# DMA transposes for the last batch's queries and two tiles of x, weight casts in blocks of 128 rows, and a new list of steps, in a fused linear-attention and highway kernel

## The chip, the core and the metric

The kernel runs on one core of a Trainium2 chip. The core has a matrix engine (TensorE, PE in the profile, with its weight loads as PEld), a vector engine (VectorE, DVE), an engine for activation functions (ScalarE, ACT), a general engine (GpSimd, POOL) and an engine that here only issues transfers (SyncE, SP). Each runs its own instructions in order, and semaphores order them against each other. Sixteen DMA engines move data between the large memory (HBM) and the on-chip SBUF. Matmul results land in PSUM.

The metric is the device time of one execution in microseconds (us), the median of several runs. The profile is of one further execution. It gives the span, from the first to the last instruction, which is a little shorter than the time.

## The reference

Linear attention over 8 batches of 8 heads, 576 positions and 64 columns a head, then a highway layer over 4608 tokens of 512 columns:

```python
def _attn_ref(q, k, v):
    q_s = np.exp(q - np.max(q, axis=-1, keepdims=True))
    q_s = q_s / (np.sum(q_s, axis=-1, keepdims=True) + 1e-09)
    k_s = np.exp(k - np.max(k, axis=2, keepdims=True))
    k_s = k_s / (np.sum(k_s, axis=2, keepdims=True) + 1e-09)
    kv = np.einsum('bhsd,bhse->bhde', k_s, v)
    return np.einsum('bhsd,bhde->bhse', q_s, kv).astype(np.float32)

def _moe_ref(x, w_h, w_t, b_t):
    H = np.maximum(x @ w_h, 0.0)
    T = 1.0 / (1.0 + np.exp(-(x @ w_t + b_t)))
    return (T * H + (1.0 - T) * x).astype(np.float32)
```

The attention's output, with its heads laid side by side, is the x of the second function. q, k, v, both 512x512 weights and the output are float32.

## The kernel before

The 4608 tokens are 36 tiles of 128 rows. Nine tiles belong to two batches: four to the first, four to the second, and one that holds the last 64 rows of each (tiles 8, 17, 26 and 35). So tiles 0 to 3 are batch 0, 4 to 7 batch 1, 27 to 30 batch 6 and 31 to 34 batch 7.

What is done is written out by hand: the string `ORDER` (L16 to L62) is a list of steps such as `mt_33_0`, where the first word is a function of the kernel, the numbers are its arguments and a letter behind a colon chooses an engine (A is ACT, D is DVE, P is POOL). The loop at the end (L491 to L494) calls the steps in this order. Each engine's own queue is therefore the list with the other engines' steps left out. Steps that only issue transfers go to SP, which takes them in order too: an issue that waits holds all issues behind it. A transfer on SP also waits for the one issued eight before it.

The steps that matter here:

- Loads: `q`, `k` and `v` of a batch, `w` (half a weight matrix, L207). Queries of batches 4 to 7 arrive in two transfers of 512 KB (`q_7_0`) and a small one for the 64 rows at the end (`q_7_9`).
- Batch steps: `ek` takes exp of k on ACT (L249) and `vc` casts v to fp16 (L255). `kv` multiplies them on PE (L261), `kr` and `kn` divide by the sums on DVE into a small matrix kvb. `eq` takes exp of the queries on ACT into a tile qe (L293). `qt` turns them on PE, with the rows on which the heads' columns then lie (L309), 8 transposes of 128x128 for two tiles of tokens, into PSUM; `qc` copies them to SBUF (L328). `turned_q` (L336) says where a tile's turned queries lie.
- Tile steps: `xu` multiplies the turned queries with kvb (L339), `rs` and `x` divide by the sums on DVE (L358, L363), which gives x in fp16. `xt` turns x on PE with four transposes (L370), `xe` copies it to SBUF (L378, DVE with D, else ACT). `bw` puts the bias into PSUM, by a matmul or, with A, by a copy on ACT (L385). `mt` and `mh` are four matmuls each with the weights t and h (L397, L405). `th` is the tanh on ACT (half the gate), `dd` is max(h, -x/2) on DVE (L428), `uu` multiplies the two, on DVE or as two instructions on POOL (L432), `oo` adds x on POOL (L453), `st` issues the store (L464).
- Weights: `whd` subtracts the identity from w_h in a block of 128 rows on POOL or DVE (L223), `whc` casts half of w_h at once with a factor 0.5 (L227), `wtc` half of w_t (L216). `fill` runs matmuls on zeros (L165).

PSUM holds two banks for gates (`ps_t`), two for h and for the halves of the first tiles (`ps_g`), one pair for kv and xu (`ps_x`) and one bank each for turned queries and turned x. So a step such as `xu` waits until `x` of the tile before has read its sums.

Of the kernel before, what the change touches and what calls it, by code (L numbers as in the profile page):

```python
# [16 lines left out]
b_0 q_0_0 v_0_1 setupdve k_0_0 b_32 eq_0_0 bsplit setuppool fill_5 fill_8 bp v_0_0 bc qt_0_0 ek_0_1 v_0_3 ek_0_0 k_0_2  # L17
v_0_2 vc_0_3:A bw_1 vc_0_0 ek_0_2 vc_0_2 q_0_4 vc_0_1:D ek_0_3 bw_0 w_h_0 fill_8 qc_0_0 whd_1:P kv_0_0 eq_0_1 w_h_2
w_t_2 kr_0_0 whd_0:P whd_2:P w_t_0 k_1_2 v_1_2 q_1_0 k_1_0 v_1_0 fill_5 q_1_4 kn_0_0 q_2_0 k_2_0 eq_0_2 xu_0_0 v_2_0
q_3_0 rs_0_0 whc_0:A x_0_0 k_3_0 fill_4 v_3_0 kv_0_1 fill_3 kr_0_1 kn_0_1 xu_0_1 rs_0_1 xu_1_0 rs_1_0 qt_0_1 x_1_0  # L20
whd_3:P qc_0_1 xt_1_0 xu_3_0 qt_0_2 xe_1_0:D fill_1 rs_3_0 x_3_0 x_0_1 xt_3_0 xu_2_0 wtc_2:P whc_2:A mh_1_0 wtc_0:P
vc_1_3 xe_3_0:D xt_0_0 xt_0_1 mh_3_0 qc_0_2:A xe_0_1 mt_1_0 mt_0_1 dd_1 ek_1_3 rs_2_0 xe_0_0:D mt_0_0 x_2_0 xt_2_0
vc_1_2:D mh_0_0 th_1_0 mh_0_1 uu_1_0 dd_3 ek_1_2 kv_1_1 dd_0 th_0_0 oo_1_0 kr_1_1 kn_1_1 bw_3 eq_1_0 bw_2 qt_1_0
uu_0_0:P xe_2_0 ek_1_1 qc_1_0 mt_3_0 xu_5_1 rs_5_1 mh_2_0 x_5_1 xt_5_1 ek_1_0 vc_1_1:A th_3_0 xe_5_1 dd_2 vc_1_0
xu_4_1 kv_1_0 mt_2_0 kr_1_0 rs_4_1 eq_1_1 bw_5 th_2_0 kn_1_0 xu_5_0 eq_1_2 q_4_0 x_4_1 rs_5_0 x_5_0 mt_5_1 xu_4_0
qt_1_1 qc_1_1:A oo_0_0 v_4_0 xt_5_0 xe_5_0:D mh_5_1 uu_3_0:P bw_4 mh_5_0 rs_4_0 x_4_0 xt_4_1 xe_4_1:D mt_5_0 uu_2_0:P
oo_2_0 eq_2_0:F th_5_0 xu_6_0 dd_5 xt_4_0 xe_4_0:D qt_1_2 mh_4_1 mt_4_1 mt_4_0 th_4_0 oo_3_0 mh_4_0 bw_8:A rs_6_0
uu_5_0:P bw_6:A qc_1_2 ek_2_0:F x_6_0 xt_6_0 xe_6_0:D oo_5_0 xu_8_0 qt_2_0 rs_8_0 mh_6_0 q_4_9 x_8_0 dd_4 xt_8_0
xe_8_0:D xu_7_0 rs_7_0 qc_2_0 x_7_0 mt_6_0 dd_6 mt_8_0 vc_2_2:A qt_2_1 th_6_0 xt_7_0 qc_2_1:A th_8_0 vc_2_0 kv_2_0
mh_8_0 xe_7_0:D uu_6_0 kr_2_0 kn_2_0 mh_7_0 k_4_0 eq_3_0:F xu_9_0 dd_8 uu_4_0:P k_5_0 bw_7 qt_2_2 v_5_0 rs_9_0 oo_4_0  # L30
x_9_0 mt_7_0 xt_9_0 dd_7 qc_2_2:A q_5_0 xu_10_0 xe_9_0:D bw_10:A th_7_0 rs_10_0 x_10_0 oo_6_0 qt_3_0 qc_3_0 mh_9_0
bw_9:A ek_3_0:F uu_8_0:P uu_7_0:P vc_3_0 xu_12_0 st_1_1 xt_10_0 oo_8_0 rs_12_0 x_12_0 xe_10_0:D oo_7_0 mt_9_0 dd_9
qt_3_1 vc_3_2:A xu_11_0 xt_12_0 rs_11_0 x_11_0 xe_12_0:D mt_10_0 th_9_0 th_10_0 kv_3_0 uu_9_0 oo_9_0 xt_11_0 mh_10_0
xe_11_0 kr_3_0 kn_3_0 dd_10 mh_12_0 qc_3_1 xu_14_0 rs_14_0 x_14_0 bw_12:A bw_11:A mt_12_0 mh_11_0 uu_10_0:P oo_10_0
xu_13_0 eq_4_0 eq_4_1 qt_3_2 st_1_0 xt_14_0 vc_4_0 mt_11_0 dd_12 rs_13_0 th_12_0 x_13_0 qc_3_2 uu_12_0:P bw_14:A
oo_12_0 xu_15_0 rs_15_0 x_15_0 xe_14_0 th_11_0 qt_4_0 dd_11 mt_14_0 uu_11_0 xt_13_0 xu_16_0 rs_16_0 qc_4_0:A xe_13_0
x_16_0 mh_14_0 qt_4_1 xt_15_0 th_14_0 bw_13:A xu_17_0 xe_15_0:D mt_13_0 rs_17_0 x_17_0 ek_4_0:F mh_13_0 xt_16_0 eq_4_2
vc_4_2 th_13_0 k_6_0 kv_4_0 dd_14 dd_13 xe_16_0:D kr_4_0 kn_4_0 bw_15:A uu_13_0 mh_15_0 ek_5_0:F bw_16:A oo_11_0
vc_5_2:A mt_15_0 th_15_0 q_5_9 qc_4_1 xu_18_0 rs_18_0 x_18_0 v_6_0 dd_15 uu_14_0:P mh_16_0 xt_17_0 xe_17_0:D qt_4_2
mt_16_0 th_16_0 vc_5_0 dd_16 kv_5_0 oo_14_0 oo_13_0 kr_5_0 kn_5_0 qc_4_2:A mh_17_0 xt_18_0 xe_18_0:D bw_17:A uu_16_0  # L40
q_6_0 mt_17_0 eq_5_0:F xu_20_0 rs_20_0 mh_18_0 st_5_0 qt_5_1 x_20_0 dd_17 xt_20_0 bw_18:A st_3_1 th_17_0 xu_21_0
st_3_0 xe_20_0:D mt_18_0 qc_5_1:A uu_15_0:P bw_20:A rs_21_0 oo_15_0 st_5_1 x_21_0 qt_5_0 xt_21_0 dd_18 q_7_0 v_7_0
th_18_0 bw_21:A st_7_1 oo_16_0 xu_19_0 ek_6_0 uu_17_0:P oo_17_0 xe_21_0:D ek_6_2 rs_19_0 mh_20_0 mh_21_0 vc_6_0:A
x_19_0 xt_19_0 qc_5_0 xe_19_0:D xu_22_0 st_7_0 rs_22_0 x_22_0 dd_20 k_7_0 dd_21 mt_20_0 th_20_0 mt_21_0 vc_6_2
uu_18_0:P xt_22_0 kv_6_0 xe_22_0:D eq_5_2 mh_19_0 bw_19:A mt_19_0 qt_5_2 kr_6_0 kn_6_0 th_21_0 uu_21_0 xu_23_0 qc_5_2
eq_6_0:F mh_22_0 st_16_1 uu_20_0:P qt_6_0 bw_22:A st_10_1 rs_23_0 x_23_0 xt_23_0 xu_24_0 st_10_0 dd_19 mt_22_0
xe_23_0:D oo_18_0 oo_20_0 th_19_0 rs_24_0 oo_21_0 x_24_0 uu_19_0:P bw_23:A dd_22 mt_23_0 oo_19_0 qc_6_0 xt_24_0
xe_24_0:D st_21_0 xu_25_0 mh_23_0 q_6_9 rs_25_0 th_22_0 uu_22_0:P oo_22_0 mh_24_0 x_25_0 xt_25_0 dd_23 xu_26_0 dd_24
rs_26_0 th_23_0 bw_24:A mt_24_0 x_26_0 eq_7_0:F uu_23_0:P qt_7_0 st_12_0 qc_7_0 xu_27_0 q_7_9 oo_23_0 rs_27_0 x_27_0
xe_25_0 mh_25_0 st_17_0 qt_6_1 qc_6_1 bw_25:A vc_7_2:A th_24_0 xt_26_0 xe_26_0:D vc_7_0:A mt_25_0 th_25_0 uu_24_0  # L50
xu_29_0 rs_29_0 x_29_0 bw_27:A st_12_1 mh_26_0 bw_26:A xt_27_0 xe_27_0:D qt_7_1 dd_25 xu_28_0 st_8_0 uu_25_0:P st_14_1
mt_26_0 rs_28_0 ek_7_0:F dd_26 mt_27_0 oo_24_0 x_28_0 xt_29_0 kv_7_0 xe_29_0:D xt_28_0 th_26_0 uu_26_0 oo_26_0 th_27_0
# [13 lines left out]
def kernel(  # L66
# [120 lines left out]
    MAIN = 4 * 2 * 4 * D  # L187

# [27 lines left out]
    def wt_cast(e, c):  # L216
        if e == "D":
            nc.vector.tensor_scalar_mul(w16["t"][:, c:c + 2], T[f"wt{c}"], 1.0)
        else:
            copy = nc.gpsimd.tensor_copy if e == "P" else nc.scalar.copy  # L220
            copy(w16["t"][:, c:c + 2], T[f"wt{c}"])  # L221
# [5 lines left out]
    def wh_cast(e, c):  # L227
        if e == "D":
            nc.vector.tensor_scalar_mul(w16["h"][:, c:c + 2], T[f"wh{c}"], 0.5)
        else:  # L230
            nc.scalar.mul(w16["h"][:, c:c + 2], T[f"wh{c}"], 0.5)
# [103 lines left out]

    def turned_q(b, jp, n):  # L336
        return T[f"eq{b}_{jp // 2}"][:, jp % 2, n]
# [16 lines left out]

    def sums(i, k):
        return T[f"xu{i}_{k}"][:, :, 0:260].rearrange("p k (s e) -> p k s e", s=4)
# [6 lines left out]
    def x(e, i, k):  # L363
        k0, k1 = heads(i, k)
        t = once(f"xn{i}", lambda: xp.tile([P, 2, 4, D], FP16, tag="x16", name=f"x16_{i}"))
        T[f"x{i}"] = t.rearrange("p k s e -> p (k s e)")
        nc.vector.tensor_mul(t[:, k0:k1], sums(i, k)[:, :, :, 0:64],  # L367
                             T[f"rs{i}_{k}"][:, 0:k1 - k0].unsqueeze(3).to_broadcast([P, k1 - k0, 4, D]))

    def xt(e, i, k):  # L370
        k0, k1 = heads(i, k)
        t = T[f"xtps{i}"] = turned[:, 0]
        for n in range(2 * k0, 2 * k1):
            n0 = n // 2 * 2 * P
            nc.tensor.matmul(t[:, n], T[f"x{i}"][:, n0 + n % 2:n0 + 2 * P:2], idh, is_transpose=True,  # L375
                             start=True, stop=True, skip_group_check=True)
# [20 lines left out]
    def mt(e, i, k):  # L397
# [3 lines left out]
        for n in parts:  # L401
            nc.tensor.matmul(T[gate(i, k)][:, cs], T[f"xT{i}"][:, n], w16["t"][:, n, cs], start=False,  # L402
                             stop=(n == parts[-1] and not first), skip_group_check=True)

    def mh(e, i, k):  # L405
# [3 lines left out]
        for n in parts:  # L409
            nc.tensor.matmul(t, T[f"xT{i}"][:, n], w16["h"][:, n], start=(first and n == parts[0]),  # L410
# [17 lines left out]
    def dd(e, i):  # L428
        t = T[f"d{i}"] = dp.tile([P, DM], FP16, tag="d16", name=f"d16_{i}")
        nc.vector.scalar_tensor_tensor(t, T[f"x{i}"], -0.5, T[f"gps{i}"], op0=ALU.mult, op1=ALU.max)  # L430
# [22 lines left out]
    def oo(e, i, h):  # L453
# [8 lines left out]
        eng.tensor_add(t[:, cs], T[f"u{i}_{h}"][:, cs], T[f"x{i}"][:, cs])  # L462
# [62 lines left out]
```

## Time and profile before

| what | value |
|---|---|
| median of 3 runs | 119.61 us (119.45 to 119.64) |
| profiled execution | 119.67 us |
| its span | 117.6 us |
| bytes moved | 40.06 MB (read 30.41, written 9.44) |
| the last real matmuls start at | 111.83 us |
| 128x512 matmuls of weights h and t, busy per instruction | 379 ns |
| transposes of 128x128 on PE, busy per instruction | 219 to 220 ns |
| qc, 128x1024 | 681 ns on DVE, 1013 on ACT |
| xe, 128x512 | 421 ns on DVE, 582 on ACT |
| x and dd, 128x512, on DVE | 690 and 678 ns |
| oo, 128x512, on POOL | 1157 ns |
| weight casts, 128x1024 | 1057 ns on ACT, 1039 on POOL |

Busy time of each engine and the load on the transfers in some stretches, as the trace gives it:

```profile
10.00:20.00 10.00, 7.79 (x94) 4.26 (x93) 7.04 (x20) 5.37 (x8) 4.47 (x7) 1.00 1.04 394
20.00:30.00 10.00, 9.34 (x131) 4.91 (x131) 7.00 (x18) 8.26 (x14) 6.92 (x9) 1.00 1.07 381
40.00:50.00 10.00, 9.83 (x152) 6.08 (x150) 9.40 (x23) 9.36 (x13) 9.70 (x11) 1.00 1.06 377
95.00:100.00 5.00, 5.00 (x39) 2.79 (x38) 4.53 (x10) 3.82 (x10) 4.84 (x6) 1.00 0.73 188
100.00:105.00 5.00, 5.00 (x41) 2.88 (x39) 4.44 (x11) 3.38 (x7) 4.83 (x7) 1.00 0.97 339
```

The columns are the stretch, its length, the busy us of PE, PEld, DVE, ACT and POOL with the number of instructions, the granted clock, the transfers' share of the sixteen engines (it can pass 1 by the way packets are counted) and GB/s. A matmul counts as busy until its modelled end, though the next one starts before it, so a PE that is busy all the time need not be at its limit; the distance between starts says more.

### The profile page before, as it was taken

To read this page: it belongs to the slowest core of one execution; us is meant where nothing else is said; L and a number is where in the kernel's file an instruction comes from. 1 tells how busy PE (TensorE), PEld (TensorE's weight loads), DVE (VectorE), ACT (ScalarE), POOL (GpSimd) and SP (SyncE) were. 2 spreads that over 40 slices of the span, in tenths; PEclk is the share of its full clock that TensorE was granted. 3 is DMA by queue.
4 is the path that set the end of the run, shared out by engine and by line. 5 is a ranking of instruction groups with operands and counts; after the bars stand their busy time and mean duration, and the time that the engine had idled before them with its cause. 6 is when DMAs were issued, how large, how long until landed. Compare 5 with 4: busy or idle time off the path is not lost.

```text
span 117.6 us, 3461 instructions
## 1 busy us (share of the span) xinstructions
PE 110.6 (94%) x1371; PEld 63.6 (54%) x1371; DVE 94.3 (80%) x223; ACT 92.3 (78%) x130; POOL 91.9 (78%) x103
## 2 busy tenths in 40 slices
PE   5999867989999999999999999999999999999991
PEld 1354443535655666556655566666666655554450
DVE  5654685588769899997899999889989898988870
ACT  4375481798999999799999999996998987774520
POOL 5022237299999999999999999899999789996860
PEclk9999999999999999999999999999999999999999
DMA  2999999999999999999999999999999977971595
GB/s 46 393 392 380 408 396 385 378 375 384 394 389 390 389 391 362 374 355 390 389 375 383 381 363 361 395 374 380 406 403 363 279 235 180 301 283 56 210 364 173
DMA packets 22083, 40.06 MB, mean 341 GB/s; under 512 B 3250, under 2 KB 9650, under 8 KB 22068
## 3 DMA queue, kind: packets, MB, share of 16 engines
q1 hardware_dynamic: 21920, 39.72, 94.8%
q8 instruction: 10, 0.16, 0.6%
q10 hardware_dynamic: 148, 0.14, 0.4%
q14 instruction: 5, 0.04, 0.1%
HBM read 30.41 MB, written 9.44 MB: 339 GB/s over the span
## 4 chain that ended last, share of the span: by engine, by line
PE 69%; DMA 17%; DVE 8%; SPq 2%; ACT 1%; issue 1%; DVEq 0%
PE gps L410 23%; PE tps L402 22%; DMA q<-in_q_dram 11%; PE xu L352 6%; DMA v<-in_v_dram 6%; PE turned L375 5%; PE kv L268 4%; DVE x L367 4%; PE qps L323 2%; PE qps L318 2%; SPq L183 2%; PE turned L167 2%; DVE d L430 2%; ACT qe L306 1%; DVE rs L361 1%
## 5 line engine op out<-in xcount | busy, mean ns | idle before, releaser
L462 POOL TENSOR_TENSOR o<-u,x 128x512 f32<-128x512 f16 (+1 forms) x36 | 40.7, 1144 | 3.7 <-DVE u L444 2.8
L402 PE MATMUL tps<-w16t,xT 128*128 128x512 f16 (+1 forms) x148 | 36.3, 373 | 0.8 <-POOL w16t L221 0.8
L410 PE MATMUL gps<-w16h,xT 128*128 128x512 f16 x144 | 36.3, 379 | 0.0
L367 DVE TENSOR_TENSOR x<-xu,rs 128x512 f16<-128x512 f32 (+1 forms) x39 | 25.2, 649 | 2.8
L442 POOL TENSOR_TENSOR u<-g,d 128x512 f16<-128x512 f16 x21 | 24.3, 1157 | 2.5 <-DVE rs L361 0.9
L430 DVE SCALAR_TENSOR_TENSOR d<-x,gps 128x512 f16<-128x512 f16 x36 | 24.2, 678 | 1.7 <-PE gps L410 1.6
L252 ACT ACTIVATE ek<-k 128x576 f16<-128x576 f32 (+2 forms) x15 | 18.0, 1222 | 2.5 <-DMA k<-in_k_dram 2.5
L402 PEld LDWEIGHTS <-xT 128*128 128x128 f16 x148 | 13.4, 98 | 12.1 <-issue 1.1
L410 PEld LDWEIGHTS <-xT 128*128 128x128 f16 x144 | 12.8, 98 | 11.4 <-DVE xT L382 0.5
L390 ACT COPY tps<-ball 128x512 f32<-128x512 f32 x28 | 16.3, 592 | 2.4 <-DVE u L444 2.1
L258 POOL CAST v<-v 128x1152 f16<-128x1152 f32 (+1 forms) x10 | 9.5, 953 | 10.4 <-DMA v<-in_v_dram 9.9
L375 PE MATMUL turned<-idh,x 128*128 128x128 f16 x144 | 14.3, 220 | 1.0 <-DVE x L367 1.0
L352 PE MATMUL xu<-kvb,eq 128*128 128x130 f16 (+1 forms) x160 | 14.8, 224 | 0.5 <-DVE eq L332 0.2
L167 PE MATMUL turned<-blank 128*128 128x512 f16 x44 | 12.5, 431 | 1.3 <-POOL blank L149 1.3
L352 PEld LDWEIGHTS <-eq 128*128 128x128 f16 (+1 forms) x160 | 10.2, 100 | 6.5 <-DVE x L367 1.3
L424 ACT ACTIVATE th<-tps 128x512 f16<-128x512 f32 x21 | 12.3, 592 | 1.6 <-PE tps L402 1.6
L375 PEld LDWEIGHTS <-x 128*128 128x128 f16 x144 | 10.1, 98 | 6.5 <-DVE x L367 2.6
L441 POOL TENSOR_SCALAR g<-th 128x512 f16<-128x512 f16 x21 | 13.1, 622 | 0.2 <-ACT th L424 0.2
L382 DVE COPY xT<-turned 128x512 f16<-128x512 f16 (+1 forms) x27 | 10.8, 399 | 2.8 <-PE turned L375 2.5
L306 ACT ACTIVATE qe<-q 128x1024 f16<-128x1024 f32 (+2 forms) x8 | 9.2, 1160 | 4.3 <-DMA q<-in_q_dram 4.1
L426 ACT ACTIVATE tps<-tps 128x512 f32<-128x512 f32 (+1 forms) x16 | 8.9, 556 | 2.9 <-PE tps L402 2.7
L444 DVE SCALAR_TENSOR_TENSOR u<-tps,d 128x512 f16<-128x512 f32 (+1 forms) x15 | 10.0, 669 | 0.8 <-ACT tps L426 0.2
(48 smaller groups left out, 114.6 us busy)
## 6 DMA issues: line engine op xcount, KB each, us to landing
k<-in_k_dram SPq DMA_DIRECT2D x6, 1152.0 KB, 11.6
v<-in_v_dram SPq DMA_DIRECT2D x6, 1152.0 KB, 14.4
out_dram<-o SPq DMA_DIRECT2D x23, 256.0 KB, 6.3
q<-in_q_dram SPq DMA_DIRECT2D x10, 512.0 KB, 9.5
out_dram<-o SPq DMA_DIRECT2D x6, 512.0 KB, 5.5
k<-in_k_dram SPq DMA_DIRECT2D x4, 576.0 KB, 11.9
q<-in_q_dram SPq DMA_DIRECT2D x2, 1152.0 KB, 15.6
q<-in_q_dram SPq DMA_DIRECT2D x2, 640.0 KB, 10.5
```

Of the source, the lines that this page charges most:

```text
L167: nc.tensor.matmul(spare, blank[:, 0:P], blank, start=True, stop=True, skip_group_check=True)
L252: nc.scalar.activation(t[:, :, c:c + n].rearrange("p j c d -> p c j d"), T[f"k32{b}"][:, c:c + n].rearrange("p c (j d) -> p c j d", j=NJ), ...
L352: nc.tensor.matmul(dst, turned_q(b, jp, n), kvb[b % NKV][:, hh, kk], start=True, stop=True, skip_group_check=True)
L367: nc.vector.tensor_mul(t[:, k0:k1], sums(i, k)[:, :, :, 0:64], T[f"rs{i}_{k}"][:, 0:k1 - k0].unsqueeze(3).to_broadcast([P, k1 - k0, 4, D]))
L375: nc.tensor.matmul(t[:, n], T[f"x{i}"][:, n0 + n % 2:n0 + 2 * P:2], idh, is_transpose=True, start=True, stop=True, skip_group_check=True)
L390: nc.scalar.copy(t[:, cs], ball[:, cs])
L402: nc.tensor.matmul(T[gate(i, k)][:, cs], T[f"xT{i}"][:, n], w16["t"][:, n, cs], start=False, stop=(n == parts[-1] and not first), skip_gro ...
L410: nc.tensor.matmul(t, T[f"xT{i}"][:, n], w16["h"][:, n], start=(first and n == parts[0]), stop=(n == parts[-1] and not (first and len(part ...
L430: nc.vector.scalar_tensor_tensor(t, T[f"x{i}"], -0.5, T[f"gps{i}"], op0=ALU.mult, op1=ALU.max)
L441: nc.gpsimd.tensor_scalar(g, T[f"th{i}"], 1.0, 1.0, op0=ALU.add, op1=ALU.mult)
L442: nc.gpsimd.tensor_mul(t, g, T[f"d{i}"])
L462: eng.tensor_add(t[:, cs], T[f"u{i}_{h}"][:, cs], T[f"x{i}"][:, cs])
```

## The change

Three parts:

- Batch 7's queries for tiles 31 to 34 are turned by two DMA transposes on SP (`qd`) straight from qe into SBUF, 128x1024 each, in place of `qt_7_0`, `qt_7_1` and their `qc`. They are cut by halves of qe, not by tiles, so `turned_q` looks elsewhere for batch 7. The small `qt_7_2` for tile 35 stays.
- x of tiles 32 and 33 is turned by a DMA transpose on SP (`xt_33_0:T`, `xt_32_0:T`), 128x512, in place of four PE transposes and the copy `xe`. For these tiles `x` writes its columns in another order in two DVE instructions, so that the blocks come out right; `dd` and `oo` read x through a view with a step of 256 elements, and `mt` and `mh` take the blocks in another order.
- `wtc` and `whc` cast one block of 128 rows (128x512) and are spread over POOL, ACT and DVE.

The list of steps is new throughout. Among other things it loads w_t ahead of w_h and batch 1's queries ahead of its k and v, runs `mt` of tiles 1, 3 and 0 ahead of `mh`, has fewer fills (26 in place of 44), more `vc` on POOL, fewer `uu` on POOL (18 in place of 21), and puts tile 6's bias on PE.

```diff
     def wt_cast(e, c):
-        if e == "D":
-            nc.vector.tensor_scalar_mul(w16["t"][:, c:c + 2], T[f"wt{c}"], 1.0)
-        else:
-            copy = nc.gpsimd.tensor_copy if e == "P" else nc.scalar.copy
-            copy(w16["t"][:, c:c + 2], T[f"wt{c}"])
+        copy = dict(D=nc.vector.tensor_copy, P=nc.gpsimd.tensor_copy).get(e, nc.scalar.copy)
+        copy(w16["t"][:, c], T[f"wt{c // 2 * 2}"][:, c % 2])
...
     def wh_cast(e, c):
...
+        mul = nc.vector.tensor_scalar_mul if e == "D" else nc.scalar.mul
+        mul(w16["h"][:, c], T[f"wh{c // 2 * 2}"][:, c % 2], 0.5)
...
+    def qd(e, b, g):
+        t = T[f"eq{b}_{g}"] = eqp.tile([P, 2, 4, P], FP16, tag="eq", name=f"eq_{b}_{g}")
+        half = MAIN // 2
+        nc.sync.dma_start_transpose(t.rearrange("p a n t -> p (a n) t"),
+                                    T[f"qe{b}"].rearrange("p j c d -> p (j c d)")[:, g * half:(g + 1) * half])
+
     def turned_q(b, jp, n):
+        if b in TURNED and jp < 4:
+            return T[f"eq{b}_{n % 2}"].rearrange("p a n t -> p (a n) t")[:, 2 * jp + n // 2]
         return T[f"eq{b}_{jp // 2}"][:, jp % 2, n]
...
+        if i in SPLIT:
+            flat = T[f"x{i}"].rearrange("p (r k s m) -> p k s m r", k=2, r=2, s=4)
+            for kk in range(2):
+                nc.vector.tensor_mul(flat[:, kk], sums(i, k)[:, kk, :, 0:64].rearrange("p s (m r) -> p s m r", r=2),
+                                     T[f"rs{i}_{k}"][:, kk].unsqueeze(2).unsqueeze(3).to_broadcast([P, 4, 32, 2]))
+            return
...
+        if e == "T":
+            t = T[f"xT{i}"] = xtp.tile([P, 4, P], FP16, tag="xT", name=f"xT_{i}")
+            nc.sync.dma_start_transpose(t, T[f"x{i}"])
+            return
...
-        nc.vector.scalar_tensor_tensor(t, T[f"x{i}"], -0.5, T[f"gps{i}"], op0=ALU.mult, op1=ALU.max)
+        nc.vector.scalar_tensor_tensor(shaped(i, t), natural(i), -0.5, shaped(i, T[f"gps{i}"]), op0=ALU.mult, op1=ALU.max)
...
+        if i in SPLIT:
+            eng.tensor_add(shaped(i, t), shaped(i, T[f"u{i}_{h}"]), natural(i))
+        else:
+            eng.tensor_add(t[:, cs], T[f"u{i}_{h}"][:, cs], T[f"x{i}"][:, cs])
```

The list's part around batch 7's queries and around the two tiles, after:

```
... eq_7_0:F v_7_0 xt_24_0 mh_23_0 x_25_0 xe_24_0:D xu_26_0 xt_25_0 bw_24:A mt_23_0 oo_19_0 qc_6_1 rs_26_0 qd_7_0 ...
... xu_33_0 rs_33_0 mt_28_0 th_28_0 x_33_0 oo_27_0 st_21_0 uu_29_0:P st_14_0 mt_31_0 uu_28_0 th_31_0 bw_30:A xt_30_0
qc_6_2:A oo_28_0 xu_32_0 st_8_0 xe_30_0:D mh_31_0 oo_29_0 rs_32_0 x_32_0 q_7_9 eq_7_2 st_23_0 dd_31 mh_30_0 xt_33_0:T
dd_30 st_17_0 uu_31_0:P oo_31_0 bw_33:A xu_34_0 qt_7_2 rs_34_0 x_34_0 qc_7_2:A xt_32_0:T st_26_0 mt_30_0 mh_33_0 ...
```

## The prediction

> **What bounds the kernel now.** I read the page's busy line and slices first, then the chain that ended last in order of time, then the stretches, then each engine's timeline at both ends of the span.
>
> ```profile
> PE 110.6 (94%) x1371; PEld 63.6 (54%) x1371; DVE 94.3 (80%) x223; ACT 92.3 (78%) x130; POOL 91.9 (78%) x103
> DMA  2999999999999999999999999999999977971595
> ```
>
> A busy PE proves little, since ends are modelled; the chain decides:
>
> ```profile
> 24.61 0.62 PE qps L323 x8
> 25.23 0.86 PE tps L402 x4
> ...
> 38.98 0.73 PE kv L268 x68
> ...
> 89.75 0.86 PE gps L410 x4
> 90.61 0.22 PE turned L375 x4
> 90.84 0.45 PE qps L318 x8
> 91.28 0.23 PE xu L352 x4
> ...
> 111.99 0.87 PE tps L402 x8
> 112.86 2.16 PE turned L167 x10
> ```
>
> From 24.61 to 112.86 the chain is almost all PE, and it gives the true spacing of starts: 0.216 us for a 128x512 matmul (0.86 for four), 0.055 for a transpose, 0.057 for an xu matmul, 0.8 for one batch's kv. Pricing every step of the list so, without fills, gives 95.7 us of PE work in the kernel before; it ends at 112.86, so 17.1 us are start, waits and slips. Behind 112.86 comes a tail of 4.74 us (last tanh, two DVE steps, a store) to the span's 117.6. The profiled execution took 119.67, 2.07 above its span; the median of the runs is 119.61.
>
> The start is set by loads:
>
> ```profile
> 13.95 0.88 POOL L225 TENSOR_TENSOR w32h<-w32h,idf 128x128 f32<-128x128 f32 x2 [2.44 <-DMA w32h<-in_moe_w_h_dram]
> 17.69 1.04 POOL L221 CAST w16t<-w32t 128x1024 f16<-128x1024 f32 x1 [1.59 <-DMA w32t<-in_moe_w_t_dram]
> 20.09 1.89 PE L402 MATMUL tps<-w16t,xT 128*128 128x512 f16 x8 [0.83 <-POOL w16t L221]
> 23.50 1.06 ACT L306 ACTIVATE qe<-q 128x1024 f16<-128x1024 f32 x1 [0.69 <-DMA q<-in_q_dram]
> ```
>
> Each wait ends on a landing. The transfers run full from 3 us (the DMA slices), so a load lands when the bytes ahead of it have: the four weight halves at 13.95, 15.2, 17.7 and 19.0, then half-MB pieces about every 1.5 us (20.5, 22.0, 23.5, 25.0, 26.6, 28.3).
>
> **The change, part by part.**
>
> *PE work.* Removed: two query turnings of batch 7 (16 transposes, 2 x 0.45) and x of tiles 32 and 33 (2 x 0.22): 1.34 us. Added: tile 6's bias goes from an ACT copy to a PE matmul, 0.22. Net -1.12: 94.6 us of work. Fills fall from 44 to 26; they stood in idle time, so this is worth nothing.
>
> *Other engines*, counted over both lists with the rows' durations: ACT loses two evictions of 128x1024 and one of 128x256 (1.01 and 0.37), five vc casts (5.3 together) and a bias copy (0.59), gains two xT copies (0.58) and ends 6.6 us lower; POOL takes six vc casts (5.9 together), gives up three g and u pairs (1.78 each), half of its weight casts and one subtraction, and ends 0.9 lower; DVE gains three u steps (0.69), two weight casts (0.55) and a subtraction (0.46), loses four xT copies (0.42) and a vc cast (0.75), and ends some 1.7 us higher. The written-out layout splits x of tiles 32 and 33 into two instructions (2 x 0.42 for 0.69: +0.15 on DVE). POOL's and DVE's reads of that layout step over 256 elements; nothing here shows such a read: between the present 1.16 us and twice that for o. I take 1.16; POOL idles 0.90, 0.45 and 0.33 before its last sums, so that most of one doubled sum would be hidden, and the second would cost up to 0.6.
>
> *Start.* The t weights now land first (13.95, 15.2) and need no subtraction; their casts are split over POOL and ACT (0.55 each, half of the 1.04 and 1.06 rows), so tile 1's gate matmuls can start near 16.7, not 20.09. The h weights land at 17.7 and 19.0, lose the identity on POOL (0.45 a block, three after one another) and DVE, and are ready at about 20.4; PE then does gps of tiles 1, 0, 3, 2 until about 24.3. By then it is 1.3 us of work ahead of before. But batch 1 still lands up to 28.3, its bytes being the same: kv needs k_1 (23.5, two exps of 0.63, so 24.8), its second half v_1 (26.6 plus a 0.67 cast, 27.3), then normalising, and the second query turning waits for q at 28.3 plus 0.41 and 1.06 of exp. I count PE dry for 0.5, 0.55, 0.7 and 0.7 us there, where before it still had tiles 3 and 2 in hand. Kv of batch 2 waits in both kernels for v_2 (issued at 23.0, 14.4 to landing: 37.4) and a cast of 1.15, so it starts near 38.7 (before: 38.98). Work ahead of it in the list: 22.6 us after, 23.5 before. So the new start only shifts work: behind kv_2 there are 72.0 us of PE work left, against 72.2.
>
> *Sum.* Before, those 72.2 us took 112.86 - 38.98 = 73.9, so 1.7 us of slips. With the same slips: 38.7 + 72.0 + 1.7 = 112.4, 0.45 earlier. The tail: dd of tile 35 now starts only after mh of tile 35, which stands later in the list, some 0.2 longer. Net -0.25: 119.67 - 0.25 = 119.4.
>
> *The DMA turnings.* The price of one is in no row. Nearest below: the last 128 KB store, alone on the rings, 2.2 us from issue to landing. Nearest above: a 256 KB store in the full stretch, 6.3 us. A gain below nothing is excluded, since the matmuls wait for the landing.
>
> ```profile
> out_dram<-o SPq DMA_DIRECT2D x23, 256.0 KB, 6.3
> out_dram<-o SPq DMA_DIRECT2D x1, 128.0 KB, 2.2
> ```
>
> Batch 7's queries have cover: exp of q_7 stands 11.8 us of PE work ahead of xu of tile 31. SP holds there for that exp, and behind it on SP stand stores alone (tile 9's and later), k_7 and v_7 having been issued, so nothing that computes starves. Tile 33 has less: between its xu and its first mh stand 5.3 us of PE work (mt 28 and 31, xt 30, xu 32, mh 31 and 30, xu 34, a short turning, mt 30). Before, x ended 1.45 us after its xu started (99.70 to 101.15); with 0.15 more, 3.7 us are left to land. I take 3 us (128 KB, transfers no longer full there), so no wait; the ends 2.2 and 6.3 give 0 to 2.6 us of waiting. Tile 32's mh comes 2.3 us of work after tile 33's and its transpose goes out one 256 KB store later, which is the same margin. Behind SP's wait for x_33 and x_32 are stores of tiles 17, 26 and 18, long computed; their delay shows only if the rings are not empty by the end.
>
> The Trainium skill ("VectorE: DVE Perf Modes", section on the three transpose paths) puts a 128x128 transpose at 1309 ns by DMA against 390 ns on TensorE, and advises TensorE where PSUM will do; if four blocks overlap that is under 3.7 us, if they run in turn it is 5.2 and an estimated wait of 1.5. Here the row gives 55 ns of PE for it, so by that page the trade looks poor; no run yet shows the DMA's side.
>
> **The rivals.**
>
> *Tiles 33 and 32 land late* (slower). SP issues them in order behind a 512 KB store, with transfers again at 339 GB/s in the stretch from 100 to 105, so 4.5 to 6.3 us is possible; PE then stands at mh of tile 33, whose whole chain follows in order. Decides from 3.7 us on. Wait 0.8 to 2.6, midway 1.5: 120.9. For: the 512 KB stores took 5.5 us from issue to landing. Against: the stretch from 95 to 100 is only 0.73 busy. Chance 0.27.
>
> *The slips go too* (faster). The 1.7 us hold 0.6 that stand where the chain leaves PE for DVE (42 to 48 and 55 to 58). ACT, POOL and DVE have 3, 5 and 0.4 us less to do behind kv_2, so waits for PSUM and casts may vanish, and half of the dry time before may be bridged: about 1 us, 118.4. Against: DVE, the engine in that chain, gains almost nothing. Chance 0.17.
>
> *PE falls back to its slow spacing at the start.* The first 13 fills take 4.69 us, 1.9 more than at 0.216; later ones run at 0.226. The new list has no fill between about 12 and 17 us, with some 2.1 us of small work in it. If the slow spacing returned, 1.9 us would be lost, of which the dry time by batch 1 hides part: +0.8, 120.2. Against: before has about as little work from 12.8 to 17.1 and stays fast. The Trainium skill ("TensorE: Matmul & The Clock Gate", Parts 1 and 4) says an idle window of some 3.4 us closes the gate and that transposes hardly count as activity; before agrees only in that it opened after 3.8 us. Chance 0.08.
>
> **How the numbers follow.** Forecast 0.48, the rivals 0.27, 0.17, 0.08. Two measurements of this kernel can be told apart from about 0.2%, 0.24 us: faster is below 119.37, slower above 119.85. The forecast's own range is 118.9 to 119.9, split 0.24 faster, 0.17 same, 0.07 slower. With the rivals: faster 0.24 + 0.17 = 0.41; same 0.17 + 0.02 from mild cases = 0.19; slower 0.40. The range reaches from 118.3 to 121.2, leaving the worst landings out.
>
> **What would show it.** Right: gates of tile 1 near 16.7, dry PE between 24 and 30, kv of batch 2 near 38.7, PE dense behind it, its last matmul near 112.4, landing of the tile transposes within 3.7 us. Wrong: PE waiting before mh of tile 33 or 32 on a DMA; kv_2 before 38 or after 39.5; a spacing of 0.43 after 12 us; xu of tile 31 waiting for its queries; DVE behind the chain for longer than before.

## The result and the profile after

| | before | after |
|---|---|---|
| median of 4 runs | 119.53 us (118.98 to 119.64) | 122.43 us (122.34 to 122.73) |
| ratio, with its 95% interval | 1 | 1.0256 (1.0219 to 1.0293) |
| span of the profiled execution | 117.6 us | 120.6 us |
| PE's last real matmuls end, as the timeline models it | 112.87 us | 115.33 us |
| the last store is issued, on ACT | 114.29 us | 116.90 us |

The changed kernel is slower by 2.9 us. Of the 3.0 us by which the spans differ, 2.46 arise before the end of PE's last matmul and the rest in the tail behind it. Busy time and slices, the page's first two parts, of the changed kernel:

```profile
PE 107.4 (89%) x1330; PEld 60.0 (50%) x1330; DVE 98.9 (82%) x227; ACT 86.5 (72%) x126; POOL 90.8 (75%) x102
...
PE   5999679987999999999999999999999995689920
...
DMA  3999999999999999999999999999999999529995
```

PE is less busy by 3.2 us and DVE more busy by 4.6, where the prediction had counted 1.7 more for DVE. ACT is 5.8 lower and POOL 1.1. A slice is 3.0 us. PE's row now has a hole in the slices that begin at 99.5 and 102.5 (5 and 6 tenths), and the transfers have one just behind it (5 and 2). The stretches say the same of these 10 us, with the columns explained for the kernel before:

```profile
95.00:100.00 5.00, 5.00 (x38) 2.72 (x36) 4.69 (x12) 3.37 (x7) 4.17 (x5) 1.00 1.00 291
100.00:105.00 5.00, 3.06 (x20) 1.34 (x17) 4.89 (x7) 2.85 (x6) 4.02 (x5) 1.00 0.73 227
```

From 100 to 105 PE works 3.06 us of 5 where before it worked all 5, and DVE is the full engine, 4.89 us with only 7 instructions. The chain of waits names them (start, us, engine, tile, line, count):

```profile
99.92 2.44 DVE x L387 x2
102.36 0.52 DVE u L471
102.88 0.33 DVE xT L409
103.20 0.13 DVE rs L378
103.38 0.04 issue
103.42 2.44 DVE x L387 x2
105.86 0.05 issue
105.91 0.41 PE xu L355 x4
```

L387 is the new way in which `x` of tiles 33 and 32 is written. The chain stays on DVE from 99.9 to 105.9. In the kernel before it ran through PE alone from 96 us on, and the xu of tiles 32 and 34 stood in it without a wait:

```profile
102.28 0.23 PE xu L352 x4
...
104.24 0.23 PE xu L352 x4
```

The groups of instructions, with shapes kept apart (busy us, mean ns of one), show how long one takes. In the kernel before, the whole x of such a tile was one instruction of 690 ns. The changed kernel:

```profile
L492 POOL TENSOR_TENSOR o<-u,x 128x512 f32<-128x512 f16 x33 | 37.7, 1155 | 3.4 <-DVE u L471 1.9 <-DMA out_dram<-o 0.7
...
L387 DVE TENSOR_TENSOR x<-xu,rs 128x256 f16<-128x256 f32 x4 | 4.9, 1406 | 0.2
L390 DVE TENSOR_TENSOR x<-xu,rs 128x256 f16<-128x256 f32 x6 | 2.5, 420 | 0.1
L490 POOL TENSOR_TENSOR o<-u,x 128x512 f32<-128x512 f16 x2 | 2.4, 1224 | 1.7 <-DVE u L471 1.6
```

The same operation on the same 128x256 takes 1.41 us at L387 and 0.42 at L390. The two of one tile overlap a little, so that a pair takes 2.44 us. The difference is the order of the columns. At L387 the results alternate between two places 256 elements apart (column 0, 256, 1, 257 and so on), while PSUM is read in order. *Reading* that layout costs almost nothing, 1.22 us against 1.16 for POOL's sum. The timeline shows who waits (in brackets, idle time of the engine just before, and what ended it):

```profile
99.92 2.44 DVE L387 TENSOR_TENSOR x<-xu,rs 128x256 f16<-128x256 f32 x2
...
102.42 0.41 PE L355 MATMUL xu<-kvb,eq 128*128 128x130 f16 x4 [1.50 <-DVE x L387]
102.42 1.25 SPq L397 DMA_TRANSPOSE xT<-x  x1
...
103.42 2.43 DVE L387 TENSOR_TENSOR x<-xu,rs 128x256 f16<-128x256 f32 x2
...
105.91 0.41 PE L355 MATMUL xu<-kvb,eq 128*128 128x130 f16 x4 [1.35 <-DVE x L387]
106.01 1.19 SPq L397 DMA_TRANSPOSE xT<-x  x1
```

The two xu are those of tiles 32 and 34. There is one pair of PSUM banks for xu, so xu of tile 32 cannot start before x of tile 33 has read its sums, and xu of tile 34 waits for x of tile 32. PE takes its queue in order and stands. Measured by the starts of matmuls, beyond the spacing that each form has when PE is dense, 1.66 and 1.52 us are lost, together 3.2. Up to 100 us, all such losses and the fills add up to 19.9 us after and 19.4 before: half a microsecond more.

The start went much as worked out. From the timeline of the first part:

```profile
15.09 1.17 POOL L218 CAST w16t<-w32t 128x512 f16<-128x512 f32 x2 [3.69 <-DMA w32t<-in_moe_w_t_dram]
...
16.92 1.03 PE L429 MATMUL tps<-w16t,xT 128*128 128x512 f16 x4
...
25.27 0.48 PE L263 MATMUL kv<-v,ek 64*64 64x65 f16 x35 [0.58 <-POOL v L253]
```

Tile 1's gates start at 16.92 (16.7 was expected), gps at 19.95 (20.4), PE runs dry at batch 1 (here for its second half of v), and kv of batch 2 starts at 38.66 (38.7).

### The profile page after: what moved, and what is told of

It reads as the page before. It is cut to its first block, busy times and chain, and to the rows that moved or that the text cites. A ratio compares the mean times of both kernels' runs of the same rounds, so it can differ in the third digit from the quotient of the medians.

```text
span 120.6 us, 3401 instructions
## 1 busy us (share of the span) xinstructions
PE 107.4 (89%) x1330; PEld 60.0 (50%) x1330; DVE 98.9 (82%) x227; ACT 86.5 (72%) x126; POOL 90.8 (75%) x102
## 2 busy tenths in 40 slices
DMA packets 25283, 40.85 MB, mean 339 GB/s; under 512 B 6450, under 2 KB 12850, under 8 KB 25268
## 4 chain that ended last, share of the span: by engine, by line
PE 47%; DVE 16%; DMA 14%; POOL 9%; issue 4%; ACT 4%; SPq 1%; DVEq 0%; ACTq 0%; POOLq 0%
PE tps L429 16%; PE gps L437 14%; DMA w32h<-in_moe_w_h_dram 9%; PE xu L355 5%; DMA v<-in_v_dram 4%; PE turned L402 4%; DVE x L387 4%; DVE d L457 4%; PE kv L263 3%; POOL u L469 3%; POOL v L253 3%; DVE u L471 2%; PE qps L313 2%; DVE x L390 2%; ACT ek L247 2%
## 5 line engine op out<-in xcount | busy, mean ns | idle before, releaser
L492 POOL TENSOR_TENSOR o<-u,x 128x512 f32<-128x512 f16 (+1 forms) x34 | 38.4, 1140 | 3.5 <-DVE u L471 1.9
L390 DVE TENSOR_TENSOR x<-xu,rs 128x512 f16<-128x512 f32 (+1 forms) x37 | 23.9, 646 | 2.6
L253 POOL CAST v<-v 128x1152 f16<-128x1152 f32 (+1 forms) x16 | 15.3, 966 | 10.7 <-DMA v<-in_v_dram 9.2
L469 POOL TENSOR_TENSOR u<-g,d 128x512 f16<-128x512 f16 x18 | 20.8, 1155 | 2.6 <-DVE d L457 1.2
L453 ACT ACTIVATE tps<-tps 128x512 f32<-128x512 f32 (+1 forms) x19 | 10.6, 561 | 7.1 <-PE tps L429 7.0
L471 DVE SCALAR_TENSOR_TENSOR u<-tps,d 128x512 f16<-128x512 f32 (+1 forms) x18 | 12.3, 686 | 2.0 <-ACT tps L453 1.1
L451 ACT ACTIVATE th<-tps 128x512 f16<-128x512 f32 x18 | 10.6, 592 | 3.2 <-PE tps L429 3.2
L301 ACT ACTIVATE qe<-q 128x1024 f16<-128x1024 f32 (+3 forms) x9 | 9.3, 1055 | 3.3 <-DMA q<-in_q_dram 3.3
L468 POOL TENSOR_SCALAR g<-th 128x512 f16<-128x512 f16 x18 | 11.1, 617 | 0.7 <-ACT th L451 0.7
L378 DVE RECIPROCAL rs<-xu 128x8 f32<-128x8 f32 (+1 forms) x39 | 7.6, 197 | 3.2 <-PE xu L355 3.2
L409 ACT COPY xT<-turned 128x512 f16<-128x512 f16 (+1 forms) x14 | 7.8, 554 | 3.2 <-PE turned L402 2.4
## 6 DMA issues: line engine op xcount, KB each, us to landing
v<-in_v_dram SPq DMA_DIRECT2D x6, 1152.0 KB, 11.6
```

Source lines behind the costliest of these rows:

```text
L253: copy(v16[b % NV][:, c:c + n, :, 0:D], T[f"v32{b}"][:, c:c + n].rearrange("p c (j d) -> p c j d", j=NJ))
L469: nc.gpsimd.tensor_mul(t, g, T[f"d{i}"])
L471: nc.vector.scalar_tensor_tensor(t[:, cs], T[gate(i, h)][:, cs], 1.0, T[f"d{i}"][:, cs], op0=ALU.add, op1=ALU.mult)
```

## The experiments

All are timed against the kernel before on the same chip, whose medians there were 119.66 to 119.72.

**x of tiles 32 and 33 written in contiguous runs.** The layout is the same and so is the work; each of the two instructions now fills one run of 256 (all even, then all odd columns) and steps through PSUM instead.

```
-flat = T[f"x{i}"].rearrange("p (r k s m) -> p k s m r", ...)
-for kk in range(2):
-    nc.vector.tensor_mul(flat[:, kk], sums(i, k)[:, kk, :, 0:64].rearrange(...), ...)
+flat = T[f"x{i}"].rearrange("p (r k s m) -> p r k s m", ...)
+for r in range(2):
+    nc.vector.tensor_mul(flat[:, r], sums(i, k)[:, :, :, r:64:2], ...)
```

> The changed kernel, with x of tiles 32 and 33 still in two instructions of 128x256, but each now writes one run of 256 neighbouring elements (the step is on the PSUM side instead). Theory, it is the write in steps of 256 elements that costs: each takes 0.42 to 0.55 us in place of 1.41, the waits of xu 32 and xu 34 on x (1.66 and 1.52 us lost) go, and the time is 122.4 - 3.1 = 119.3. Rival one, two instructions are dear as such, or stepping in PSUM is as dear: x stays above 1 us and the time above 121.5. Rival two, the tile transposes themselves hold PE: the waits move to mh 33 and mh 32 and the time stays above 120.5.

Measured: 119.94 us (119.27 to 121.21), ratio 1.0019 (0.9987 to 1.0051), 2.5 us under the changed kernel and 0.6 over the 119.3 expected. The group of these instructions by shape, and the two waits that are now the largest of that stretch, from the timeline:

```profile
L387 DVE TENSOR_TENSOR x<-xu,rs 128x256 f16<-128x256 f32 x4 | 1.5, 420 | 0.2
```

```profile
104.17 0.28 PE L318 MATMUL qps<-idh,qe 128*128 128x128 f16 x2 [0.68 <-ACT qe L292]
...
106.00 1.04 PE L437 MATMUL gps<-w16h,xT 128*128 128x512 f16 x4 [0.69 <-DMA xT<-x]
```

One instruction takes 0.42 us again (0.76 for the pair), and the waits of xu are gone. Behind them a new one appears, the landing of tile 33's transpose (issued at 101.52 right behind a store of 512 KB, 4.43 us until PE could go on), and one for the small load of batch 7's queries, which stands late on SP. Each costs 0.85 us by the starts of matmuls in this execution, which was 0.92 longer than the median.

**The layout alone, in the kernel before.** The old list, old casts and PE transposes stay; only x of tiles 32 and 33 is written, and later read, in the new layout.

```
+SPLIT = (32, 33)
...
+flat = T[f"x{i}"].rearrange("p (r k s m) -> p k s m r", ...)
...
-nc.tensor.matmul(t[:, n], T[f"x{i}"][:, n0 + n % 2:n0 + 2 * P:2], idh,
+nc.tensor.matmul(t[:, n], T[f"x{i}"][:, cols], idh,
```

> The kernel before, its list and its PE transposes, with nothing but the layout of x for tiles 32 and 33: x in two instructions that write in steps of 256 elements, dd and oo that read so, PE transposes that read neighbouring columns. Theory: x of each takes 2.44 us as in the changed kernel; xu 32 waits 0.8 us and xu 34 about 1.0 more, 121.3 to 122.0. Rival, the new list or the DMA transposes are the cause: within 0.3 of 119.5.

Measured: 122.52 us (122.15 to 122.54), ratio 1.0229 (1.0186 to 1.0271). By shape:

```profile
L384 DVE TENSOR_TENSOR x<-xu,rs 128x256 f16<-128x256 f32 x4 | 4.9, 1399 | 0.2
L387 DVE TENSOR_TENSOR x<-xu,rs 128x256 f16<-128x256 f32 x6 | 2.5, 422 | 0.2
```

The layout alone makes the kernel before as slow as the whole change did, by 2.9 us, more than the 121.3 to 122.0 expected. Its profile shows where the time goes: 0.93 us lost before the turning of tile 33, which in the old list stands ahead of xu of tile 32, and 2.01 before xu of tile 34.

```profile
102.95 0.28 PE L396 MATMUL turned<-idh,x 128*128 128x128 f16 x2 [0.77 <-DVE x L384]
...
107.04 0.41 PE L352 MATMUL xu<-kvb,eq 128*128 128x130 f16 x4 [1.84 <-DVE x L384]
```

Put in, the layout costs; with the layout kept and the order of writing changed, the cost goes: x as it is written is the cause. d reads x in the same alternating order, and d of tiles 33 and 32 in the changed kernel takes what every d takes:

```profile
108.55 0.68 DVE L457 SCALAR_TENSOR_TENSOR d<-x,gps 128x512 f16<-128x512 f16 x1
...
111.17 0.68 DVE L457 SCALAR_TENSOR_TENSOR d<-x,gps 128x512 f16<-128x512 f16 x1
```

The mean of all d there, 685 ns against 678 before, is higher mainly because of one d of another tile, right behind the slow x, that counts as 890 ns. So reading in this order is free on DVE. The contiguous form also walks PSUM and the row sums in another order than the slow form; no run separates that from the write, and that the write is what costs in the instruction is inferred from d. The Trainium skill ("SBUF — State Buffer", the note on SBUF cachelines in the section on the DMA port swizzle) says that consecutive accesses run at full rate while they stay in one line of 16 bytes, and that every one that crosses to another pays. The write agrees: 256 results, each 512 bytes from the one before, cost 1406 - 420 = 986 ns more, 3.9 ns each. The reads do not: d is as fast, and POOL's sum takes 1224 instead of 1155 ns. The Trainium skill's "GPSIMD Engine Reference" (section on performance pitfalls for Q7 kernels) puts half as much again on reads that step over more than 8 bytes; POOL's sum here pays 6%.

**Tiles 32 and 33 turned on PE again, queries still by DMA,** in the new list, with plain x.

```
-xt_33_0:T ... xt_32_0:T
+xt_33_0 xe_33_0:D ... xt_32_0 xe_32_0:A
```

> The changed kernel with x of tiles 32 and 33 whole and turned on PE again (xe 33 on DVE, xe 32 on ACT); batch 7's queries stay with the DMA. Theory: 0.44 us of PE work more than with the run-wise x and no wait on x: 119.4 to 119.9. Rival, the new list or the queries' DMA transposes cost the 3 us: above 121.5.

Measured: 119.98 us (119.51 to 120.78), ratio 1.0036 (1.0002 to 1.0070). The same as the first experiment: turning the two tiles by DMA wins nothing beyond noise, once x is written cheaply.

**All DMA turnings in the old list,** with the cheap x and the old casts; each transpose of queries stands where its PE step stood, and each of x right behind x.

```
-qt_7_0 st_12_0 qc_7_0 ... qt_7_1 ... xt_33_0 xe_33_0:D ... xt_32_0 ... xe_32_0
+qd_7_0 st_12_0 ... qd_7_1 ... x_33_0 xt_33_0:T ... x_32_0 xt_32_0:T
```

> The list and the weight casts of before, with all DMA transposes put in where their PE steps stood (queries) and right behind x (tiles 33 and 32), and x written in runs. Theory, the transposes are worth the PE work they save where nothing else is lost: 119.5 less up to 1.3, so 118.2 to 118.7. Rival, they land too late in a list made without them (2.4 us from issue, against some 2.5 us between x 32 and its mh): 119.3 or more. Second rival, SP held by its wait for exp of q_7 delays stores that free buffers: 119.5 to 120.5.

Measured: 127.67 us (126.38 to 130.12), ratio 1.0625 (1.0569 to 1.0682). The profiled execution is the longest of these runs, so its waits are read for their places. From the timeline, and then one of the stretches (the third number from the end is the granted clock, which was 1.00 from 93 to 97):

```profile
97.89 0.23 PE L361 MATMUL xu<-kvb,eq 128*128 128x130 f16 x1 [1.14 <-DMA eq<-qe]
101.11 0.51 PE L361 MATMUL xu<-kvb,eq 128*128 128x130 f16 x3 [3.00 <-DMA eq<-qe]
115.56 1.57 PE L443 MATMUL gps<-w16h,xT 128*128 128x512 f16 x4 [2.49 <-DMA xT<-x]
```

```profile
101.00:105.00 4.00, 3.89 (x13) 1.74 (x14) 1.49 (x3) 1.39 (x3) 0.46 (x1) 0.50 0.58 218
```

In these places of the old list the landings are waited for three times. The clock drops as well: in the second of these waits, at 98.9 us (granted 0.86 from 98.5 to 99.0), it fell to 0.50 and stayed there until 105.7, so that four matmuls of 128x512 took 1.71 us instead of 0.86. It fell again at 115.9, 0.4 us after the end of the wait of 2.49. The Trainium skill ("TensorE: Matmul & The Clock Gate", Part 1) puts the idle window that closes the gate at some 3.4 us. Read as one unbroken wait, this trace does not agree: 1.14 us of waiting, a matmul, and some 0.75 of the next wait were enough, and then 2.49 alone, while the changed kernel's two waits of 1.50 and 1.35 left the clock at 1.00.

**SP's order, in the repaired kernel,** with a second measurement of the latter beside it. The small load of batch 7 goes up to that of batch 6, and the 512 KB store of tile 23 goes behind both tile transposes.

```
-q_6_9 oo_26_0 ... x_32_0 q_7_9 eq_7_2 st_23_0 dd_31 ... xt_33_0:T ... xt_32_0:T
+q_6_9 q_7_9 oo_26_0 ... x_32_0 eq_7_2 dd_31 ... xt_33_0:T ... xt_32_0:T st_23_0
```

> The same kernel as the one whose x of tiles 32 and 33 writes contiguous runs, again beside the others of this call. Its first profiled execution took 120.86, 0.92 above its median, and lost 0.85 us before the short turning of batch 7 and 0.85 before mh of tile 33. If these two losses are what separates its long executions from its short ones, an execution near 119.9 shows about 0.8 of the two together; if they are always there, both show again.

> Theory: what is left over in the repaired kernel is SP's order around tiles 33 and 32. With the small load of batch 7's queries issued right behind that of batch 6, and the 512 KB store put behind both tile transposes, the waits before the short turning and before mh of tile 33 fall below 0.2 us, and the time comes 0.6 to 1.2 us under the repaired kernel's, 118.8 to 119.4. Rival: the transposes land late because of their own time or of the transfers already under way; then the wait before mh of tile 33 stays at 0.5 or more, the time is 119.6 to 120.0.

Measured: the repaired kernel again 120.26 us (119.59 to 121.80), ratio 1.0039 (1.0012 to 1.0065); with the new order 121.02 (120.49 to 121.22), ratio 1.0103 (1.0078 to 1.0127). The repaired kernel's profiled execution here was 121.80, with 1.30 and 1.18 us lost at the same two places. So the two waits stand in both profiles and are larger in the longer execution; no profile near the median is at hand. In the new order both waits are gone, as the theory had it, and still the kernel is slower: a miss. PE's last matmul started earlier, at 112.4 (113.9 in the first profile of the repaired kernel), but now the stores ended the execution. SP stood before x of tile 33 from 98.97 to 101.27 with stores behind it, and at the end POOL waited 0.73 and 0.74 us, and DVE 0.30, for earlier stores to land before they could write the last sums.

**Only the first of the two edits.** The 512 KB store stays ahead of the transpose.

```
-x_32_0 q_7_9 eq_7_2
+q_6_9 q_7_9 ... x_32_0 eq_7_2
```

> The repaired kernel with one edit of two: the small load of batch 7's queries is issued right behind that of batch 6; the 512 KB store stays ahead of tile 33's transpose. Theory: the kernel with both edits was slow because SP stood idle with empty rings from 98.97 to 101.27, the store behind the wait for x of tile 33, so that the stores reach into the tail; with the store ahead the rings stay fed, the wait before the short turning goes, that before mh of tile 33 stays at 0.7 to 1.2, and the time is 119.3 to 119.9. Rival: any order that keeps the tile transposes on SP ends in the stores, and the time is 120.3 to 121.

Measured: 120.57 us (119.48 to 121.78), ratio 1.0061 (1.0030 to 1.0092), inside the rival's range. Its profiled execution, 119.65, is nearer to the theory: nothing is lost at the turning, and before mh of tile 33 only 0.31 us, less than the 0.7 to 1.2 expected. The times spread over 2.3 us, and what makes the long ones long is not in that profile: inconclusive.

**The same edit with tiles 32 and 33 on PE.**

```
-xt_33_0:T ... xt_32_0:T
+xt_33_0 xe_33_0:D ... xt_32_0 xe_32_0:A
...
-q_6_9 ... q_7_9
+q_6_9 q_7_9
```

> The kernel with tiles 32 and 33 turned on PE and only batch 7's queries by DMA (119.98), with the small load of batch 7's queries issued right behind that of batch 6. Theory: no wait of SP for x is left, so the stores flow, and the waits around the short turning (0.3 to 0.6) go: 119.3 to 119.8. Rival: that load was on no critical path there, and the time stays at 119.9 to 120.1.

Measured: 120.16 us (119.64 to 121.89), ratio 1.0051 (1.0022 to 1.0080). No gain: the load was not what set that kernel's time.

**The list and the casts alone.** Nothing is turned by DMA.

```
-qd_7_0 ... qd_7_1 ... xt_33_0:T ... xt_32_0:T
+qt_7_0 qc_7_0 ... qt_7_1 qc_7_1 ... xt_33_0 xe_33_0:D ... xt_32_0 xe_32_0:A
```

> The new list and the casts by block alone: batch 7's queries and tiles 32 and 33 are turned on PE as before. Theory: PE's list of work sets the end, so the 16 transposes put back cost their 0.9 us over the kernel with only the tiles on PE (119.98): 120.6 to 120.9, 0.9 to 1.2 slower than the kernel before; the new start then is a loss of about 1 us. Rival: PE has room there (waits for PSUM and for kv of batch 7 absorb them) and the time stays 119.8 to 120.2.

Measured: 121.59 us (121.53 to 122.35), ratio 1.0167 (1.0142 to 1.0193). Slower than expected by 0.7. The query turnings cost 1.6 us here, not the 0.9 of their work on PE; their places in the list were chosen by hand for this run, and their copies add two instructions to DVE, so that 0.7 of it may be the placing. It is left open. The profiled execution does not decide it: it took 0.8 more than the median and started late. Its fills stay 0.427 us apart until 10.2 us (until 5.1 in the changed kernel), and tile 1's gates start at 18.84 instead of 16.92.

**Queries on PE, tiles by DMA,** in the kernel with SP's new order.

```
-qd_7_0 ... qd_7_1
+qt_7_0 qc_7_0 ... qt_7_1 qc_7_1
```

> The kernel with SP's order changed, with batch 7's queries back on PE, and only tiles 32 and 33 turned by DMA. Theory: it costs the 0.9 us of PE work that the query transposes saved, less what their two long holds of SP (1.3 and 2.6 us of issuing) delay: 0.5 to 0.9 over the kernel with SP's order changed. Rival: the holds of SP cost as much as PE gains; then the two are within 0.2 us of each other.

Measured: 123.02 us (122.84 to 123.06), ratio 1.0275 (1.0254 to 1.0295), 2.0 over the kernel with the queries by DMA: outside both expectations. Without the query transposes SP is done early and comes to x of tile 33 long before it is there. Two stretches, and SP's longest wait:

```profile
95.00:100.00 5.00, 4.71 (x28) 2.23 (x27) 4.71 (x12) 3.40 (x7) 4.37 (x5) 1.00 0.14 49
100.00:105.00 5.00, 5.00 (x42) 3.01 (x41) 4.79 (x13) 3.52 (x8) 4.79 (x6) 1.00 0.12 26
```

```profile
SPq L397 <- DVE x L387: 8.9, 1, 8.9
```

For 10 us the rings carry 49 and 26 GB/s while stores of tiles long done stand behind SP's wait of 8.9 us. PE's last matmul starts at 113.7, yet the last store lands at 120.3.

**The same with three stores ahead of that wait.**

```
-st_8_0 ... xt_33_0:T dd_30 st_17_0 ... xt_32_0:T st_23_0 st_26_0
+st_8_0 st_17_0 st_23_0 st_26_0 ... xt_33_0:T dd_30 ... xt_32_0:T
```

> The kernel with batch 7's queries on PE and the tiles turned by DMA (123.02), with three stores of tiles long computed (17, 23 and 26, 1.25 MB) put ahead of SP's wait for x of tile 33 and no other edit. Theory: SP waited 8.9 us there while the rings ran empty (49 and 26 GB/s from 95 to 105), and the stores behind it ended the execution; 1.25 MB take about 3.3 us at 380 GB/s, so that the tail goes back to 4.3 to 5 us behind PE's last matmul (113.8) and the time comes 2 to 3 us down, 120.2 to 121.0, with no wait before mh of tile 33. Rival: the tail is set by the issuing of the last stores on SP (0.5 to 1.2 us each) or by POOL's sums; then the time stays above 122.3.

Measured: 120.53 us (120.41 to 121.32), ratio 1.0082 (1.0053 to 1.0111), 2.5 us less for moving three issues. The same stretches:

```profile
95.00:100.00 5.00, 4.71 (x28) 2.24 (x27) 4.71 (x12) 3.41 (x7) 4.37 (x5) 1.00 0.63 228
100.00:105.00 5.00, 5.00 (x42) 3.00 (x41) 4.79 (x13) 3.55 (x8) 4.79 (x6) 1.00 0.27 79
```

PE's busy time is the same to the hundredth, and what differs is the transfers. So a DMA transpose that waits on SP can cost the tail what the rings do not carry meanwhile.

**The query transposes alone, in the kernel before.** Both stand right behind exp of q_7, the two small loads ahead of them and one 512 KB store behind.

```
-q_6_9 ... eq_7_0:F ... qt_7_0 ... qc_7_0 ... q_7_9 ... qt_7_1 ... qc_7_1
+q_6_9 q_7_9 ... eq_7_0:F qd_7_0 qd_7_1 st_21_0 ...
```

> The kernel before, with nothing of the change but batch 7's query turnings by DMA, both issued right behind the exp of q_7 (85.7 in the profile of before), the small loads of batches 6 and 7 ahead of them and one 512 KB store behind them. Theory: PE's list sets the end, so 16 transposes less are worth up to 0.9 us, less 0.3 for 0.5 MB more of DMA work: 118.7 to 119.3. Rival: behind the transfers already queued the second one lands after 97, when xu of tile 31 needs it, or the stores held up by 4 us of issuing keep the o buffers busy; then it is 119.6 to 121.

Measured: 119.31 us (118.87 to 119.71), ratio 0.9972 (0.9949 to 0.9995). It is the one version that is faster than the kernel before, by 0.3%, with an interval that only just leaves out no change. The issues, from the timeline of SP, and the slices of the transfers:

```profile
85.62 7.12 SPq L340 DMA_TRANSPOSE eq<-qe  x2
```

```profile
DMA  2999999999999999999999999999999899999695
```

The two transposes hold SP for 7.1 us and land in time: no xu waits for them. So the old list does take the query transposes, if they are issued early. Of the 0.9 us less work on PE, 0.75 is lost again in two new waits of xu for x of the tile before (0.37 before the xu at 86.5 and 0.38 before that at 90.9). PE's last matmul ends only 0.12 us earlier than in the kernel before, so that most of the 0.37 gained is not explained by PE. The lows that the kernel before had near the end, the slices 7, 1 and 5, are now 9, 9 and 6.

## Why the prediction was wrong

The forecast was 119.4 and the range 118.3 to 121.2; the time was 122.43. Taken apart by the experiments, each step against the one above it (us):

| step | forecast | measured |
|---|---|---|
| list and casts alone, against before | +1.1 | +1.9 |
| queries of batch 7 by DMA | -0.9 | -1.6 |
| tiles 32 and 33 by DMA, x written cheaply | -0.4 | 0.0 to +0.3 |
| x written in steps of 256 elements | 0 | +2.2 to +2.5 |

The first column is the forecast's sum with PE's removed work put back (119.4 and 0.9 and 0.44). The second is the differences of the medians above. The first two rows share one measurement, that of the list alone; the 0.7 to 0.8 by which they miss in opposite directions is one open question.

- **The step that failed** is in the part on other engines: "The written-out layout splits x of tiles 32 and 33 into two instructions (2 x 0.42 for 0.69: +0.15 on DVE)". The price was taken from a row of the same shape with another order of writing. Measured, the pair takes 2.44 us instead of the 0.84 counted, 1.6 more per tile. The prediction noticed that nothing in the trace showed such a layout, bounded the *reads* on both sides, and gave the *write* no bound at all. By all that the runs show it was the write that cost, and not the reads (1.22 for 1.16 on POOL, 0.68 for 0.68 on DVE).
- **Its place was missed too.** The 0.15 was booked on DVE, as if beside the path. But x frees the one PSUM pair for the next xu, and PE's queue stands behind it; two waits of 1.66 and 1.52 us followed. With a price of 1.6 that chain would have been a rival. These waits account for the whole miss: from the start of kv of batch 2 to PE's end the sum had 73.7 us (72.0 of work and 1.7 of slips); it took 76.7, and without the two waits 73.5.
- **The start** was right in its times: gates at 16.92, kv of batch 2 at 38.66, and up to 100 us half a microsecond more lost than before, against 1.1 us less work on PE. The list by itself came out 0.8 slower than the sum has it; with the hand-set places of the query turnings in that run, this stays open.
- **The other engines' work** came out apart from x: ACT 5.8 us lower (6.6 forecast), POOL 1.1 lower (0.9), and DVE 4.6 higher, of which 3.2 is x above its price. The terms that the prediction names add up to 7.1 for ACT and 1.5 for DVE, not to its 6.6 and 1.7; nothing hangs on it.
- **The landing of the tile transposes** was right in size, 2.4 us from issue in the changed kernel, where the 512 KB store had gone out 2.4 us earlier, and 3 had been taken. The rival *Tiles 33 and 32 land late* did not decide here, because x was late already; it appears as soon as x is repaired, with 0.85 us (1.18 in a longer execution), inside the 0.8 to 2.6 given for it. Its own reason, the 512 KB store ahead, is borne out in part: with the small load moved up 0.31 us of the wait were left, and with that store moved behind as well it was gone.
- **SP behind the wait for x** was put down as harmless unless the rings are not empty by the end. In the changed kernel SP waits 3.3 us there in all, and the transfers' hole is seen in the slices. That it can decide is shown by the two kernels that differ in three stores only.
- **The query transposes** had the cover claimed: they landed at 89.45 and 94.27, and no xu waited. Alone, in the kernel before and issued earlier, they gained 0.4 us of the 0.9 counted.
- **The tail**, 0.2 longer by the order of dd and mh of tile 35, came out as far as it was reckoned: from PE's last matmul to the last issue it took 1.57 us instead of 1.42. From there to the end of the span it took another 0.3 more, which no term had.
- **The other rivals.** *The slips go too* did not happen: behind kv of batch 2 the time without the two waits was 73.5 us, where the same slips give 73.7. *PE falls back to its slow spacing* did not happen in the changed kernel: tile 1's four matmuls at 16.92 stand 0.216 us apart. The clock's row of the page could not have shown it, since it stands at 9 in the first slices too, where the fills are 0.427 apart. The spacing from which the prediction judged is 0.216 in the later fills; its 0.226 is that of the first in a group. That the fills stay slow until 10.2 us in one profile of the list alone shows that the rival was not idle.

On the price of a DMA transpose, the Trainium skill's "VectorE: DVE Perf Modes" (three transpose paths) has 1309 ns for a block of 128x128. Four blocks landed in 2.4 us from their issue, and 1.2 of that was SP's issuing, so here the blocks overlap. The same page of the Trainium skill (rules for kernel authors) prefers TensorE where PSUM will do. That is borne out for the two tiles (nothing won) and not for the queries (0.4 us won in the old list, 1.6 in the new one, of which 0.7 is open).

## What to carry to other kernels

Price an instruction by its access pattern, not by its shape: when the order of the output changes, the row of the same shape is no bound, and the nearest rows on both sides must be sought for the write as well as for the reads. Then ask what the instruction frees: a step on a side engine that releases the only buffer of the bounding engine is on the path, however short it was. An issue that waits for late data belongs behind all issues whose data are ready, or the rings run dry and the stores come back at the end.

## What the runs showed of the hardware

- A DVE instruction whose fp16 results alternate between two places 256 elements apart takes 1.41 us for 128x256, against 0.42 for contiguous ones; stepping by two in PSUM on the reading side (the repaired x) costs nothing, 0.42.
- A DMA transpose from SBUF to SBUF keeps SP for 1.2 to 1.5 us for 128x512 (2.4 once, in the old list) and for 1.3 to 4.8 us for 128x1024. It lands 2.4 to 4.6 us after its issue in the one case and 4.0 to 11.6 in the other. Each tile counts as 0.14 MB and 544 more packets (25283 with both tiles by DMA, 24195 with none of them).
- The granted clock fell to half at 98.9 us in the old list with all transposes, 2.1 us after PE first stood and with one short matmul in between.
